# Inputs of the first two superblocks turned by VectorE inside a paired buffer, written to DRAM and read back in four parts, without TensorE transposes

## The chip, the core and the metric

The kernel runs on one core of one Trainium2 chip. The metric is device time in microseconds, of one execution: before the change 371.51 us, the median of 3 runs (371.48 to 371.51). Inputs, outputs and the reference are float32.

## What is computed

`S, D, F` are 2048, 512 and 1376. The two parts of one block, each with a normalisation that is scaled and shifted by a condition `c`:

```python
mod = (_silu(c) @ w_mod).reshape(c.shape[0], 6, 1, -1)
sa, ca, ga, sb, cb, gb = (mod[:, i] for i in range(6))
h = _layernorm(x) * (1 + ca) + sa                      # rows of 512
X = rfft2(h, axes=(-2, -1)) * (w_r + 1j * w_i)         # over S and D
x = x + ga * irfft2(X, s=(S, D), axes=(-2, -1))
h = _layernorm(x) * (1 + cb) + sb
h = einsum("bsd,df->bsf", h, w1) + b1
x = x + gb * einsum("bsf,fd->bsd", mish(h), w2)
```

## The kernel before, in words

**Stages.** The 2048 rows are held as 16 row groups: group `n` is row `p * 16 + n` on partition `p`, in `x[:, n, :]`. The Fourier part is done as dense products: forward over the row groups, then per frequency with the weights, then back. The way back has two steps for each group: `p3_col(n)` (eight products with `kc`, L830 and L831, and an evacuation by ScalarE, L833) and `p3_row(n)` (four products with `kiv`, L840, and an addition into `x` by VectorE, L843). `row_squares` and `row_scale` make the statistics of the second normalisation from it.

**The dense part.** Four groups make a superblock `i` (0 to 3) of 512 rows, two groups a block `b` (0 to 7). The rows must stand with D on the partitions, so a superblock's normalised rows are transposed. The transposed input is named by its quarters B11, B21, B12, B22 (first digit: the half of D; second: the block). It is scaled and shifted by the condition (`cols`), and each quarter is split into a high and a low half of type fp32r (`split_in`: a cast by ScalarE, L821, then a subtraction by VectorE, L822) so that three products (`TERMS`) give float32 accuracy. `up` (L962, and L945 for the 512 wide form) multiplies with the parts of `w1`, `evict` adds the bias and applies Mish, `down` (L1062) multiplies with `w2`. Superblock 0 uses plain products for most of F, the others a scheme of seven products for eight (`PRODUCTS`), whose input sums T1 to T4 are made in `sum_in`. After a block's last `down`, `gather` and `chain` (L1092 and after) put its sums into `modr`, `residual` (L1113) multiplies with the gate, and a DMA from POOL's queue adds the result into `x` in SBUF (L1114), from where `store` writes it out. `modr` is one buffer, used by one block after the other.

**How a superblock's input is turned.** `norm_one(n)` writes the normalised rows of group `n` into a buffer (ScalarE).

- Superblocks 0 and 1: `transpose_in` (L765) does four TensorE transposes against the identity `ident` into a PSUM bank, `scale_in` (L772) brings them to SBUF with scale and shift by ScalarE, two instructions of 128x256. `first_in` (L1184) and `next_in` (L1282) call these for a quarter.
- Superblocks 2 and 3: `turn_one` (L783) transposes in 32x32 blocks on VectorE into rows of `x` that are free again, `turn_out` (L787) writes this to DRAM from POOL's queue in four DMAs, `turn_in` (L794) reads it back turned through SyncE's (SP's) queue, and `scale_turned` (L798) scales it in place.

**Order.** Every engine runs its instructions in the order of the program. The steps of the back transform and of the dense part are entered in a `Plan` with a due time each, are sorted by it, and then run in the order that the table `ORDER` gives: 1155 steps before, 1187 after. The table is replaced as a whole by the change.

**Buffers and queues.** `buf(tag)` gives the next of two 128x512 buffers of that tag. DMAs are issued by SP (loads of `w1` and `w2`, sums of `w1` kept in DRAM by `keep_w1` (L735) and fetched again, turned reads, most stores), by POOL (accumulating `x<-modr`, turned writes) and a few by ScalarE. A queue's engine issues in program order, and what has to wait for data holds up what is behind it.

Of the kernel before, what the change touches and what calls it, by code (L numbers as in the profile page):

```python
# [81 lines left out]
def tile_spectral_block(ctx: ExitStack, tc: tile.TileContext, x_d, w1_d, b1_d, w2_d,  # L82
# [30 lines left out]

    def buf(tag, dt=F32):
        return work.tile([P, 512], dt, name="buf", tag=tag)
# [580 lines left out]
    even = [pm.tile([P, 512], F32, name=f"even{i}") for i in range(3)]  # L696
# [4 lines left out]
    ring, raws, src, temps, stage, turned = {}, {}, {}, {}, {}, {}  # L701
# [63 lines left out]
    def transpose_in(n, g):  # L765
        st["pt2"] = ps = bank("D")
        for k in range(2):
            for i in range(2):
                nc.tensor.transpose(ps[:, (2 * k + i) * P:(2 * k + i + 1) * P],
                                    st["h2", n + i][:, (2 * g + k) * P:(2 * g + k + 1) * P], ident)  # L770

    def scale_in(b, g, dst):  # L772
        raws[b] = dst
        ps = st.pop("pt2")
        for e in range(2):
            k = 2 * g + e
            nc.scalar.activation(dst[:, 256 * e:256 * e + 256], ps[:, 256 * e:256 * e + 256],
                                 AF.Identity, bias=cols[:, 1, 0, k:k + 1], scale=cols[:, 1, 1, k:k + 1])

# [13 lines left out]

    def turn_in(b, n, g):  # L794
        raws[b] = dst = buf("ty"["B12 B22".find(b) >= 0])
        nc.sync.dma_start(dst.rearrange("p (a s) -> p a s", a=4), turned[n][:, :, 128 * g:128 * g + 128])

    def scale_turned(b, g):  # L798
        for e in range(2):
            k, o = 2 * g + e, raws[b].rearrange("p (a k s) -> p k a s", a=4, k=2)[:, e]  # L800
            nc.scalar.activation(o, o, AF.Identity, bias=cols[:, 1, 0, k:k + 1], scale=cols[:, 1, 1, k:k + 1])
# [4 lines left out]
    def sum_in(b, dst=None):  # L806
        p, q, op = {"T1": ("B12", "B11", ALU.subtract), "T2": ("T1", "B22", ALU.subtract),
                    "T3": ("B22", "B12", ALU.subtract), "T4": ("B21", "T2", ALU.add)}[b]
        p, q = raws[p], raws[q]
        raws[b] = raws[dst] if dst in raws else dst if dst is not None else buf("h")  # L810
        nc.vector.tensor_tensor(raws[b], p, q, op=op)

    def split_in(b, i=0):
# [4 lines left out]
        if i > 1:  # L818
            r = r.rearrange("p (a m j) -> p m a j", a=4, m=4)
            h, l = (z.rearrange("p (m a j) -> p m a j", a=4, m=4) for z in (h, l))  # L820
        nc.scalar.copy(h, r)  # L821
# [50 lines left out]
    def load_w2(t, spare=None):  # L872
        st["w2", t] = rs = []
        for e, f, rows in tiles(t):
            r = buf("y")[:rows] if spare is None else spare[:, e]
# [312 lines left out]
    for n, s in ((0, 5), (1, 6), (2, 8), (3, 9)):  # L1188
        plan.at(s - N2 + 0.7, norm_one, n)
# [303 lines left out]
```

## Time and profile before

| | |
|---|---|
| median of 3 runs | 371.51 us |
| time of the profiled execution | 371.68 us |
| its span, first to last instruction | 369.9 us |
| mean granted TensorE clock | 0.998 |
| TensorE matmuls (PE), weight loads (PEld) | 361.9 us, 337.5 us |
| VectorE (DVE) | 298.3 us |
| ScalarE (ACT) | 266.8 us |
| GpSimd (POOL) | 73.9 us |
| moved by DMA | 85.76 MB |

Busy times are sums over the span of 369.9 us. They are averages over stages, so the stretches are looked at one by one: the back transform and the first superblock's input lie at 90 to 134 us, the second superblock's input is turned up to 168 us. In a row of grouped instructions stand the line of the kernel, the engine, the operation, out<-in, then durations in ns as least/median/greatest, and the first and last start. A timeline row has start, duration and count. The chain of waits has start and duration of each link. For DMA issues, "to landing" is the time from the issuing instruction to the last byte's arrival.

### The profile page before, as it was taken

What the parts mean: (1) busy time and instruction counts of PE and PEld (TensorE: products, weight loads), DVE (VectorE), ACT (ScalarE), POOL (GpSimd) and SP (SyncE); (2) the same over time, 40 slices, a digit from 0 to 9 for tenths busy, and PEclk for the clock granted to TensorE, in tenths of its full rate; (3) what the DMA queues carried; (4) which work ended last, traced back from release to release, by engine and by line L of the source; (5) the groups of instructions that cost most, each with busy time, mean ns of one, the idle gap of its engine ahead of it and who ended that gap; (6) DMA issues with size and microseconds to landing.
All of it is one profiled execution on the core that took longest, in us unless ns stands there. A gap on an engine that the chain in (4) does not pass through costs nothing. (4 is left out here: it accounts for less than half of the span.)

```text
span 369.9 us, 7822 instructions
## 1 busy us (share of the span) xinstructions
PE 361.9 (98%) x2698; PEld 337.5 (91%) x2698; DVE 298.3 (81%) x744; ACT 266.8 (72%) x601; POOL 73.9 (20%) x118
## 2 busy tenths in 40 slices
PE   8999999998999999999999999999989999999995
PEld 8999977777999999888999999999979999999994
DVE  1898967888887678989987489996749887588996
ACT  1698879996899989998757587775776654455750
POOL 0488738786000000000011210004100000000000
PEclk9999999999999999999999999999999999999999
DMA  7999997778634847657988779779896597870423
GB/s 251 381 345 378 346 371 226 230 186 307 217 115 171 257 153 221 249 196 244 259 196 265 275 246 271 239 215 280 268 232 178 170 274 265 239 269 2 116 57 113
DMA packets 49351, 85.76 MB, mean 232 GB/s; under 512 B 7169, under 2 KB 16481, under 8 KB 49057
## 3 DMA queue, kind: packets, MB, share of 16 engines
q1 hardware_dynamic: 45376, 72.56, 59.2%
q0 software_dynamic: 1776, 5.77, 7.2%
q10 hardware_dynamic: 2160, 6.95, 6.3%
q8 instruction: 21, 0.34, 0.4%
q14 instruction: 18, 0.14, 0.1%
HBM read 66.12 MB, written 15.47 MB: 221 GB/s over the span
## 5 line engine op out<-in xcount | busy, mean ns | idle before, releaser
L962 PE MATMUL bank<-hT,wr 128*128 128x256 f32 x360 | 52.3, 283 | 0.0
L1114 POOL DMA_DIRECT2D x<-modr x7 | 6.4, 918 | 206.2 <-DVE hT L822 97.4
L962 PEld LDWEIGHTS bank<-hT,wr 128*128 128x128 f32 x360 | 47.3, 192 | 0.2
L962 PE MATMUL bank<-hB,wr 128*128 128x256 f32 x318 | 45.2, 283 | 0.0
L962 PEld LDWEIGHTS bank<-hB,wr 128*128 128x128 f32 x318 | 41.5, 191 | 0.5
L888 DVE TENSOR_TENSOR al<-buf,ah 128x512 fp32r<-128x512 f32 (+1 forms) x45 | 30.0, 669 | 8.5 <-ACT ah L887 8.5
L1062 PE MATMUL bank<-w2a,ah 128*128 128x256 f32 x161 | 34.9, 283 | 0.0
L1062 PE MATMUL bank<-w2b,ah 128*128 128x256 f32 x147 | 32.2, 283 | 0.0
L887 ACT CAST ah<-buf 128x512 fp32r<-128x512 f32 (+1 forms) x45 | 26.7, 604 | 7.6 <-PE bank L1062 4.8
L1062 PEld LDWEIGHTS bank<-w2a,ah 128*128 128x128 f32 x161 | 27.0, 191 | 0.5
L1062 PEld LDWEIGHTS bank<-w2b,ah 128*128 128x128 f32 x147 | 25.1, 192 | 0.7
L830 PE MATMUL bank<-kc,d 128*128 128x128 f32 x128 | 24.8, 276 | 0.5 <-ACT d L440 0.5
L831 PE MATMUL bank<-kc,d 128*128 128x128 f32 x128 | 24.7, 275 | 0.0
L945 PE MATMUL bank<-hB,wr 128*128 128x512 f32 x96 | 24.7, 394 | 0.0
L1062 PE MATMUL bank<-w,ah 128*128 128x256 f32 x112 | 22.2, 287 | 1.1 <-DVE modr L1092 1.1
L302 PE MATMUL bank<-buf,mring 128*128 128x512 f32 x48 | 20.6, 430 | 0.2 <-DVE buf L295 0.2
L1062 PEld LDWEIGHTS bank<-w,ah 128*128 128x128 f32 x112 | 17.9, 191 | 2.5 <-DVE modr L1092 1.3
L830 PEld LDWEIGHTS bank<-kc,d 128*128 128x128 f32 x128 | 19.4, 192 | 0.7 <-ACT d L440 0.7
L945 PEld LDWEIGHTS bank<-hB,wr 128*128 128x128 f32 x96 | 17.1, 189 | 2.8
L831 PEld LDWEIGHTS bank<-kc,d 128*128 128x128 f32 x128 | 19.4, 192 | 0.0
L596 PEld LDWEIGHTS bank<-kv,a_sb 128*128 128x128 f32 x126 | 15.5, 191 | 2.7 <-issue 2.2
L790 POOL DMA_DIRECT2D turned<-x x16 | 8.9, 570 | 44.2 <-DVE x L784 31.9
(296 smaller groups left out, 1096.8 us busy)
## 6 DMA issues: line engine op xcount, KB each, us to landing
wr<-w_S SPq DMA_DIRECT2D x60, 256.0 KB, 3.8
wr<-w_A SPq DMA_DIRECT2D x45, 256.0 KB, 3.8
w_S<-hT SPq DMA_DIRECT2D x20, 256.0 KB, 2.2
x<-in_A_x_dram SPq DMA_DIRECT2D x16, 256.0 KB, 4.8
xring<-in_x_t_dram SPq DMA_DIRECT2D x16, 256.0 KB, 4.7
w_A<-wr SPq DMA_DIRECT2D x15, 256.0 KB, 2.7
x<-modr POOLq DMA_DIRECT2D x7, 512.0 KB, 5.8
out_dram<-x SPq DMA_DIRECT2D x7, 512.0 KB, 3.6
```

Source lines behind the costliest of these rows:

```text
L302: nc.tensor.matmul(pa, m[:, a, 0:128], g, start=(i == 0), stop=False)
L596: nc.tensor.matmul(pd[:, i * P:(i + 1) * P], y[:, i * P:(i + 1) * P], kv[:, 0:128], start=True, stop=True)
L790: nc.gpsimd.dma_start(t[:, a].rearrange("(c i) s -> i c s", c=4), x[32 * a:32 * a + 32, row:row + 2, :].rearrange("i r d -> i (r d)") .rea ...
L830: nc.tensor.matmul(o, dj[:, 0:128], kc[0][:, n, :], start=True, stop=False)
L831: nc.tensor.matmul(o, dj[:, 64:192], kc[1][:, n, :], start=False, stop=True)
L887: nc.scalar.copy(h, r)
L888: nc.vector.tensor_tensor(l, r, plain(h), op=ALU.subtract)
L945: nc.tensor.matmul(ups[i, t, f], ring[t, a][:, p, b, :], sides[int(a[2]) - 1][:, :, q, b, :], start=(a[2] == "1" and b == 0 and n == 0), s ...
L962: nc.tensor.matmul(o, w[:, p, k, :], h[:, q, k, :], start=(first and n == 0), stop=(last and n == 5), skip_group_check=True)
L1062: nc.tensor.matmul(out_ps[b][n][:, 256 * half:256 * half + 256], a[p][:, e], w2[t][q][:, r], start=(t == 1 and half == 0 and i == 0), stop ...
L1114: nc.gpsimd.dma_start(x[:, 2 * b:2 * b + 2, :], r, accum_op=ALU.add)
```

## The change

The tags `t` and `y` of `buf` become paired buffers: `wide(tag)` is one tile of 128x2x512, whose halves `buf` hands out in turn. The three `even` tiles become one, `evens`, so that two neighbours can be used as a pair. For superblocks 0 and 1 `transpose_in`, `scale_in`, `first_in` and `next_in` are gone. In their place:

- `turn_near(n)`: VectorE transposes the normalised group in 32x32 blocks into one half of the paired buffer of its block (`NEAR`: `wide("t")`, `evens[:, 0:2]`, `wide("t")`, `wide("y")` for the pairs 0 to 3).
- `send(n)`: POOL's queue writes that half (128x512, 256 KB) to DRAM.
- `turn_back(pair, c)`, for `c` from 0 to 3: SP's queue reads 32 partitions (32x8x128, 128 KB, in pieces of 512 bytes) back into the same paired buffer, now with D on the partitions.
- `scale_turned(b, g, True)`: ScalarE scales and shifts a quarter in place, in two instructions of 128x8x32, whose pieces of 32 elements come from a strided view (`in_order`). `split_in` and `sum_in` read the quarters through views of that kind.

Counted over the program, TensorE has 32 transposes fewer, VectorE 8 transposes (128x512) more, ScalarE the same number of scalings (16, formerly from PSUM), POOL's queue 8 DMAs more and SP's 16 more. The due times of the added steps are set in `near_in`, and the new `ORDER` moves steps on every engine throughout the dense part.

```diff
 ORDER = (
-    "3-4 0-2 16 21 5 7 15 14 73 38 8 10 71 47 9 75 80 12 32 62 6 26 17 19 13 31 24 22 69 20 23 82 11 33 124 87 27 "
...
+    "0 3-4 1-2 16 15 5 7 21 90 47 56 88 8 10 12 92 6 64 19 79 38 13 24 14 96 11 17 20 22 27 23 29 98 18 33 32 9 54 "
...
+    def wide(tag):
+        if tag not in wides:
+            wides[tag] = work.tile([P, 2, 512], F32, name="wide", tag=tag, bufs=1)
+        return wides[tag]
+
     def buf(tag, dt=F32):
+        if tag in "ty":
+            uses[tag] = uses.get(tag, 1) + 1
+            return wide(tag)[:, uses[tag] % 2]
         return work.tile([P, 512], dt, name="buf", tag=tag)
...
-    even = [pm.tile([P, 512], F32, name=f"even{i}") for i in range(3)]
+    evens = pm.tile([P, 3, 512], F32, name="even")
+    even = [evens[:, i] for i in range(3)]
...
-    def transpose_in(n, g):
-        st["pt2"] = ps = bank("D")
-        for k in range(2):
-            for i in range(2):
-                nc.tensor.transpose(ps[:, (2 * k + i) * P:(2 * k + i + 1) * P],
-                                    st["h2", n + i][:, (2 * g + k) * P:(2 * g + k + 1) * P], ident)
-
-    def scale_in(b, g, dst):
...
+    NEAR = {0: lambda: wide("t"), 1: lambda: evens[:, 0:2], 2: lambda: wide("t"), 3: lambda: wide("y")}
+
+    def turn_near(n):
+        pair = n // 2
+        if n % 2 == 0:
+            near[pair] = NEAR[pair]().rearrange("p n d -> p (n d)")
+        nc.vector.transpose(near[pair][:, n % 2 * D:n % 2 * D + D].rearrange("p (c k j) -> p c k j", c=4, k=4),
+                            st.pop(("h2", n)).rearrange("p (k c j) -> p c k j", k=4, c=4))
+
+    def send(n):
+        if n % 2 == 0:
+            turned[n] = dram.tile([2 * P, D], F32, name=f"turned{n}")
+        at = n % 2 * P
+        nc.gpsimd.dma_start(turned[n - n % 2][at:at + P], near[n // 2][:, n % 2 * D:n % 2 * D + D])
+
+    def turn_back(pair, c):
+        t = turned[2 * pair].rearrange("(m i) (c s) -> c i m s", i=32, c=4)
+        nc.sync.dma_start(near[pair][32 * c:32 * c + 32].rearrange("p (m s) -> p m s", m=8), t[c])
...
-    def scale_turned(b, g):
+    def in_order(r, near):
+        return r.rearrange("p a (k j) -> p k a j", k=2) if near else r.rearrange("p (a k s) -> p k a s", a=4, k=2)
+
+    def scale_turned(b, g, near=False):
         for e in range(2):
-            k, o = 2 * g + e, raws[b].rearrange("p (a k s) -> p k a s", a=4, k=2)[:, e]
+            k, o = 2 * g + e, in_order(raws[b], near)[:, e]
...
     def load_w2(t, spare=None):
...
-            r = buf("y")[:rows] if spare is None else spare[:, e]
+            r = wide("y")[:rows, e] if spare is None else spare[:, e]
...
-    def first_in(b, n, g):
-        transpose_in(n, g)
-        scale_in(b, g, buf("g2") if b in ("B11", "B21") else even[1 if b == "B12" else 0])
...
+    def near_in(n0, u, norms, ins, lag):
+        for n, s in enumerate(norms):
+            plan.at(u + s, norm_one, n0 + n)
+            plan.at(u + s + 0.3, turn_near, n0 + n)
+            plan.at(u + s + 0.35, send, n0 + n)
+        for n, s in zip((0, 2), ins):
+            for c in range(4):
+                plan.at(u + s + 0.01 * c, turn_back, (n0 + n) // 2, c)
+            for g in range(2):
+                plan.at(u + s + lag + 0.1 * g, scale_turned, f"B{g + 1}{n // 2 + 1}", g, True)
+
+    near_in(0, -N2, (4.7, 5.2, 7.7, 8.2), (6, 9), 1.2)
...
-            for b, n, g, s in (("B11", 0, 0, 17), ("B21", 0, 1, 18), ("B12", 2, 0, 23), ("B22", 2, 1, 25)):
-                plan.at(u + s + 0.3, next_in, b, 4 * i + n, g)
+            near_in(4, u, (17, 18, 23, 25), (19.5, 27), 3)
```

TensorE around the first `up` products, before. L840 is a row step, L830 and L831 the eight products of a column step, L962 an `up` of superblock 0 (its operand `hB` is a pair of quarters); L945 is the 512 wide `up`. The column step shown is the last one:

```order
352 L840 MATMUL bank<-kiv,buf 128x128 x4
353 L830 MATMUL bank<-kc_1104,d_756 128x128
354 L831 MATMUL bank<-kc_1132,d_756 128x128
355 L830 MATMUL bank<-kc_1104,d_756 128x128
356 L831 MATMUL bank<-kc_1132,d_756 128x128
357 L830 MATMUL bank<-kc_1104,d_756 128x128
358 L831 MATMUL bank<-kc_1132,d_756 128x128
359 L830 MATMUL bank<-kc_1104,d_756 128x128
360 L831 MATMUL bank<-kc_1132,d_756 128x128
361 L962 MATMUL bank<-hB_1283,wr 128x256 x12
362 L945 MATMUL bank<-hB_1283,wr 128x512 x3
```

The same place after, where `up` is L991 and L974 and the row step L869; row 350 is the row step of group 13, and the last column step begins at row 351:

```order
344 L860 MATMUL bank<-kc_1116,d_750 128x128
345 L991 MATMUL bank<-hB_1261,wr 128x256 x6
346 L974 MATMUL bank<-hB_1261,wr 128x512 x3
347 L991 MATMUL bank<-hB_1262,wr 128x256 x6
348 L991 MATMUL bank<-hB_1261,wr 128x256 x6
349 L974 MATMUL bank<-hB_1261,wr 128x512 x3
350 L869 MATMUL bank<-kiv,buf 128x128 x4
351 L859 MATMUL bank<-kc_1088,d_750 128x128
```

Six matmuls with B12, and after them products with B22 and B12, now stand ahead of the last column step; before, the first product with B12 stood behind it.

ScalarE at the input of superblock 0, before. L777 is a scaling out of PSUM, L821 the cast of a split, L833 the evacuation of a column step, L847 and L848 the row statistics, L726 a cast of `w1`:

```order
236 L833 COPY buf<-bank 128x512
237 L726 CAST hT_1339<-hT_1338 128x256
238 L777 ACTIVATE even_1281<-bank,cols 128x256 x2
239 L847 ACTIVATE mv<-mv 128x1
240 L848 ACTIVATE bank,mv<-x,mv 128x512
241 L833 COPY buf<-bank 128x512
242 L847 ACTIVATE mv<-mv 128x1
243 L848 ACTIVATE bank,mv<-x,mv 128x512
244 L777 ACTIVATE even_1280<-bank,cols 128x256 x2
245 L821 CAST hB_1284<-buf 128x512
246 L726 CAST hT_1339<-hT_1338 128x256
247 L821 CAST hB_1283<-even_1281 128x512
```

And after, where L825 is `scale_turned`, L850 the cast of a split, L862 the evacuation and L739 the cast of `w1`:

```order
236 L825 ACTIVATE wide<-wide,cols 128x8x32 x2
237 L862 COPY buf<-bank 128x512
238 L825 ACTIVATE wide<-wide,cols 128x8x32 x2
239 L739 CAST hT_1311<-hT_1310 128x256
240 L850 CAST hB_1261<-wide 128x512
241 L862 COPY buf<-bank 128x512
242 L825 ACTIVATE even<-even,cols 128x8x32 x2
243 L739 CAST hT_1311<-hT_1310 128x256
244 L825 ACTIVATE even<-even,cols 128x8x32 x2
245 L850 CAST hB_1262<-wide 128x512
246 L850 CAST hB_1261<-even 128x512
247 L850 CAST hB_1262<-even 128x512
```

The scalings of the four quarters stand close together behind the reads, with the four casts in among them and right behind, and the row statistics are no longer between them.

POOL's queue in the dense part, before: L1114 is a block's accumulation, L790 a turned write of superblock 2 or 3:

```order
95 L1114 DMA x<-modr 128x1024
96 L790 DMA turned_2754<-x 32x4x256 x4
97 L790 DMA turned_2959<-x 32x4x256 x4
98 L1114 DMA x<-modr 128x1024
99 L790 DMA turned_3417<-x 32x4x256 x4
100 L790 DMA turned_3504<-x 32x4x256 x4
101 L1114 DMA x<-modr 128x1024 x5
```

And after, with L805 for `send`, L1143 for the accumulation and L788 for the turned writes:

```order
96 L805 DMA turned_1432<-wide 128x512 x2
97 L805 DMA turned_1476<-even 128x512 x2
98 L805 DMA turned_1903<-wide 128x512 x2
99 L805 DMA turned_1987<-wide 128x512 x2
100 L1143 DMA x<-modr 128x1024
101 L788 DMA turned_2698<-x 32x4x256 x4
102 L788 DMA turned_2879<-x 32x4x256 x4
103 L1143 DMA x<-modr 128x1024
104 L788 DMA turned_3361<-x 32x4x256 x4
105 L1143 DMA x<-modr 128x1024
106 L788 DMA turned_3463<-x 32x4x256 x4
107 L1143 DMA x<-modr 128x1024 x4
```

Eight writes are added at the head, and the third accumulation, which stood behind all turned writes, now stands ahead of the last group of them.

More of the change, by code (lines that the diff above doesn't have):

```diff
@@ L112, in bank @@
         return psum.tile([P, 512], F32, name="bank", tag=tag)
+    wides, uses = {}, {}
+    def wide(tag):
+        if tag not in wides:
+            wides[tag] = work.tile([P, 2, 512], F32, name="wide", tag=tag, bufs=1)
+        return wides[tag]
     def buf(tag, dt=F32):
+        if tag in "ty":
+            uses[tag] = uses.get(tag, 1) + 1
+            return wide(tag)[:, uses[tag] % 2]
         return work.tile([P, 512], dt, name="buf", tag=tag)
@@ L700, in tile_spectral_block @@
     wsum = pm.tile([P, 512], F32, name="wsum")
-    ring, raws, src, temps, stage, turned = {}, {}, {}, {}, {}, {}
+    ring, raws, src, temps, stage, turned, near = {}, {}, {}, {}, {}, {}, {}
     def flat2(t):
@@ L763, in norm_one @@
         st["h2", n] = norm(n, True)
-    def transpose_in(n, g):
-        st["pt2"] = ps = bank("D")
-        for k in range(2):
-            for i in range(2):
-                nc.tensor.transpose(ps[:, (2 * k + i) * P:(2 * k + i + 1) * P],
-                                    st["h2", n + i][:, (2 * g + k) * P:(2 * g + k + 1) * P], ident)
-    def scale_in(b, g, dst):
[L773 to L778, printed above, removed]
     def turning(row):
@@ L792, in turn_out @@
                               .rearrange("i (c s) -> i c s", c=4))
+    NEAR = {0: lambda: wide("t"), 1: lambda: evens[:, 0:2], 2: lambda: wide("t"), 3: lambda: wide("y")}
[13 more added lines that the diff above has]
+        nc.sync.dma_start(near[pair][32 * c:32 * c + 32].rearrange("p (m s) -> p m s", m=8), t[c])
+        if c == 3:
+            v = near[pair].rearrange("p (m g s) -> p g m s", m=8, g=2)
+            for g in range(2):
+                raws[f"B{g + 1}{pair % 2 + 1}"] = v[:, g]
     def turn_in(b, n, g):
-        raws[b] = dst = buf("ty"["B12 B22".find(b) >= 0])
+        raws[b] = dst = wide("ty"["B12 B22".find(b) >= 0])[:, g]
         nc.sync.dma_start(dst.rearrange("p (a s) -> p a s", a=4), turned[n][:, :, 128 * g:128 * g + 128])
-    def scale_turned(b, g):
+    def in_order(r, near):
+        return r.rearrange("p a (k j) -> p k a j", k=2) if near else r.rearrange("p (a k s) -> p k a s", a=4, k=2)
+    def scale_turned(b, g, near=False):
         for e in range(2):
-            k, o = 2 * g + e, raws[b].rearrange("p (a k s) -> p k a s", a=4, k=2)[:, e]
+            k, o = 2 * g + e, in_order(raws[b], near)[:, e]
             nc.scalar.activation(o, o, AF.Identity, bias=cols[:, 1, 0, k:k + 1], scale=cols[:, 1, 1, k:k + 1])
@@ L809, in sum_in @@
         p, q = raws[p], raws[q]
-        raws[b] = raws[dst] if dst in raws else dst if dst is not None else buf("h")
+        raws[b] = raws[dst] if dst in raws else buf("h")
+        if len(p.shape) > len(raws[b].shape):
+            raws[b] = raws[b].rearrange("p (a s) -> p a s", a=8)
         nc.vector.tensor_tensor(raws[b], p, q, op=op)
@@ L820, in split_in @@
             h, l = (z.rearrange("p (m a j) -> p m a j", a=4, m=4) for z in (h, l))
+        else:
+            r = in_order(r, True)
+            h, l = (z.rearrange("p (k a j) -> p k a j", a=8, k=2) for z in (h, l))
         nc.scalar.copy(h, r)
@@ L1182, in tile_spectral_block @@
     plan.at(5.4 - N2, single_w1, False)
-    def first_in(b, n, g):
-        transpose_in(n, g)
-        scale_in(b, g, buf("g2") if b in ("B11", "B21") else even[1 if b == "B12" else 0])
-    for n, s in ((0, 5), (1, 6), (2, 8), (3, 9)):
-        plan.at(s - N2 + 0.7, norm_one, n)
-    for b, n, g, s in (("B11", 0, 0, 7), ("B21", 0, 1, 8), ("B12", 2, 0, 10), ("B22", 2, 1, 11)):
-        plan.at(s - N2 + 0.55, first_in, b, n, g)
+    def near_in(n0, u, norms, ins, lag):
[6 more added lines that the diff above has]
+                plan.at(u + s + 0.01 * c, turn_back, (n0 + n) // 2, c)
+            for g in range(2):
+                plan.at(u + s + lag + 0.1 * g, scale_turned, f"B{g + 1}{n // 2 + 1}", g, True)
+    near_in(0, -N2, (4.7, 5.2, 7.7, 8.2), (6, 9), 1.2)
     for b, key in (("B11", -6.6), ("B21", -5.6), ("B12", -0.5), ("B22", 0.6)):
@@ L1280, in tile_spectral_block @@
     plan.at(key, finish)
-    def next_in(b, n, g):
-        transpose_in(n, g)
-        scale_in(b, g, buf("ty"["B12 B22".find(b) >= 0]))
     for i in range(1, NB // 2):
@@ L1288, in tile_spectral_block @@
         if i == 1:
-            for n, s in ((0, 14.5), (1, 15.5), (2, 19.5), (3, 20.5)):
-                plan.at(u + s, norm_one, 4 * i + n)
-            for b, n, g, s in (("B11", 0, 0, 17), ("B21", 0, 1, 18), ("B12", 2, 0, 23), ("B22", 2, 1, 25)):
-                plan.at(u + s + 0.3, next_in, b, 4 * i + n, g)
+            near_in(4, u, (17, 18, 23, 25), (19.5, 27), 3)
         else:
```

86 rows, old and new, of the table ORDER are left out of this document.

## The prediction, made before the changed kernel was run

> **What bounds the kernel now.** I read the page first, then the busy time by stretches, the chain that ended last, and the instructions around the transposes.
>
> ```profile
> span 369.9 us, 7822 instructions
> PE 361.9 (98%) x2698; PEld 337.5 (91%) x2698; DVE 298.3 (81%) x744; ACT 266.8 (72%) x601; POOL 73.9 (20%) x118
> ```
>
> TensorE (PE) has work in 361.9 of 369.9 us. Where its 8.0 idle microseconds lie is in the table by stretches: first the stretch, then for each engine busy time and instructions, then granted clock, DMA share, GB/s.
>
> ```profile
> 10.00:90.00 80.00, 78.49 (x527) 65.14 (x526) 69.12 (x165) 69.24 (x163) 57.11 (x91) 1.00 0.92 311
> 90.00:134.00 44.00, 43.75 (x391) 43.75 (x392) 32.80 (x96) 38.62 (x104) 1.35 (x1) 1.00 0.57 189
> 134.00:168.00 34.00, 34.00 (x207) 29.85 (x206) 31.04 (x85) 32.34 (x78) 0.00 (x0) 1.00 0.59 199
> 168.00:184.00 16.00, 16.00 (x113) 14.96 (x112) 15.54 (x37) 12.60 (x27) 0.00 (x0) 1.00 0.90 270
> 184.00:260.00 76.00, 76.00 (x613) 74.66 (x612) 59.71 (x149) 52.64 (x108) 10.87 (x18) 1.00 0.83 251
> 260.00:280.00 20.00, 18.95 (x142) 17.77 (x141) 13.32 (x35) 14.09 (x30) 0.95 (x1) 1.00 0.86 241
> ```
>
> The columns are PE, weight loads, VectorE (DVE), ScalarE (ACT), POOL. From 90 to 260 us PE idles 0.25 us in all: there every matmul taken out should shorten the kernel by the time it holds PE, as long as nothing else comes late. But DVE and ACT are close behind. From 134 to 168 they work 31.04 and 32.34 of 34 us, so cover is thin exactly where the change adds VectorE work.
>
> The one stall behind 90 us is in 260 to 280: 20.00 - 18.95 = 1.05 us. The chain of waits names it, and the DVE timeline beside it shows what stood between.
>
> ```profile
> 267.19 7.54 DMA x<-modr
> 275.59 0.62 PE bank L1062 x3
> ```
> ```profile
> 265.26 1.22 DVE L1113 TENSOR_TENSOR modr<-modr 128x1024 f32<-128x1024 f32 x1
> 266.40 0.28 DVE L1032 TENSOR_TENSOR buf<-even 128x128 f32<-128x128 f32 x1
> 270.52 0.28 DVE L1032 TENSOR_TENSOR buf<-even,buf 128x128 f32<-128x128 f32 x1
> 274.84 0.69 DVE L1092 TENSOR_TENSOR modr<-bank,buf 128x512 f32<-128x512 f32 x1 [4.03 <-DMA x<-modr]
> ```
>
> The residual of block 2 leaves `modr` at 265.26 + 1.22 = 266.48; its accumulating DMA is done at 267.19 + 7.54 = 274.73, and only then may the chain of block 3 write `modr`. DVE had 11 instructions to do meanwhile, done by 270.80, then waited 4.03 us.
>
> **Removed: 32 transposes on PE.** They stand in seven runs of four or eight (L769). What a run costs is the distance from its start to the next matmul's start.
>
> ```profile
> 108.22 0.60 PE L769 MATMUL bank<-ident,buf 128*128 128x128 f32 x4
> 108.66 0.39 PE L830 MATMUL bank<-kc,d 128*128 128x128 f32 x2
> 152.05 0.60 PE L769 MATMUL bank<-ident,buf 128*128 128x128 f32 x4
> 152.40 0.48 PE L1062 MATMUL bank<-w,ah 128*128 128x256 f32 x2
> 155.63 0.60 PE L769 MATMUL bank<-ident,buf 128*128 128x128 f32 x4
> 155.98 0.94 PE L945 MATMUL bank<-hB,wr 128*128 128x512 f32 x3
> 163.40 1.04 PE L769 MATMUL bank<-ident,buf 128*128 128x128 f32 x8
> 164.19 0.48 PE L1062 MATMUL bank<-w2a,ah 128*128 128x256 f32 x2
> L769 PE MATMUL bank<-ident,buf x32: 270/272/273, 108.2 to 164.2; 128*128 128x128 f32 x32
> ```
>
> The four runs of superblock 0 cost 0.44 each, here read from the first; those of superblock 1 cost 0.35, 0.35 and 0.79. The sum is 4 x 0.44 + 1.49 = 3.25 us. All of it lies in stretches where PE is full, so all of it is on the path.
>
> The last row above says 272 ns for one transpose, but within a run they start 0.11 us apart: a duration is not what PE is held. [...] The starts of the next matmuls decide for 3.25.
>
> **Replaced: ACT scales, DVE turns.**
>
> ```profile
> L784 DVE STREAM_TRANSPOSE x<-buf x8: 670/704/711, 199.6 to 254.1; 128x512 f32<-128x512 f32 x8
> L801 ACT ACTIVATE buf<-buf,cols x16: 586/590/614, 217.0 to 271.2; 128x256 f32<-128x256 f32 x16
> L777 ACT ACTIVATE buf<-bank,cols x12: 545/557/580, 110.3 to 165.4; 128x256 f32<-128x256 f32 x12
> ```
>
> The 16 scalings stay on ACT but read SBUF: 16 x (590 - 557) ns = 0.5 us more. DVE gets 8 transposes x 0.704 = 5.6 us, and nothing is taken from it. From 90 to 168 us DVE then has 32.80 + 31.04 + 5.6 = 69.4 us of work and ACT 38.62 + 32.34 + 0.5 = 71.5, in 78 - 3.25 = 74.75 us of PE. Both still fit, ACT at 96%. This costs nothing as long as PE's work hides it; if the cover is gone, ACT's idle time there sets the pace (a rival below).
>
> **Added: the way through DRAM.** Eight writes on POOL's queue, sixteen reads of 128 KB on SP's. Nearest rows are those of the later superblocks, issue and landing for write and read.
>
> ```profile
> L790 POOL DMA_DIRECT2D turned<-x x16: 550/570/615, 202.2 to 256.9; - x16
> DMA to landing us min/median/max: 3.2/4.2/6.0
> L796 SPq DMA_DIRECT2D buf<-turned x8: 518/542/1406, 209.0 to 261.9; - x8
> DMA to landing us min/median/max: 3.4/4.3/5.0
> 106.81 5.41 SPq L735 DMA_DIRECT2D w_S<-hT  x2
> 133.11 1.68 PE L962 MATMUL bank<-hB,wr 128*128 128x256 f32 x12
> 104.65 1.06 PE L840 MATMUL bank<-kiv,buf 128*128 128x128 f32 x8
> 107.33 1.06 PE L840 MATMUL bank<-kiv,buf 128*128 128x128 f32 x8
> ```
> ```profile
> L843 DVE SCALAR_TENSOR_TENSOR x<-bank,x 128x512 f32<-128x512 f32 x16 | 11.0, 687 | 4.7 <-PE bank L840 4.7
> L821 ACT CAST hB<-buf 128x512 fp32r<-128x512 f32 x14 | 8.4, 614 | 0.3 <-PE bank L945 0.3
> L822 DVE TENSOR_TENSOR hB<-buf,hB 128x512 fp32r<-128x512 f32 x14 | 9.3, 685 | 1.9 <-ACT hB L821 1.8
> L726 ACT CAST hT<-hT 128x256 fp32r<-128x256 f32 x16 | 6.4, 406 | 0.0
> ```
>
> POOL has nothing else to do here (1.35 us busy in 90 to 134), so issue costs nothing. SP issues in order, and a read waits there for its two writes; behind it stand the kept weight sums, the loads of `w2` and later of `w1`, for which DVE waits. The tightest user is the first `up` with B12. In the new order it comes ahead of the last column step (the 2.68 us between the two L840 rows less the row step's 108.22 - 107.33 = 0.89, so 1.79) and of one row step more, so PE reaches it at 133.11 - 1.79 - 0.89 - 4 x 0.44 = 128.7.
>
> Now the pair n = 2, 3. DVE turns n = 3 right behind the evacuation of row step 5, which leaves PE at 107.33 + 0.89 = 108.2: 108.2 + 0.69 + 0.70 = 109.6. The write lands at 109.6 + 0.57 + 4.2 = 114.4. SP is free by then: the kept sum ahead of the reads is made just behind row step 7, two steps of 2.68 later, about 114. Four issues of 0.54 and 4.3 to landing give 120.9. ACT reaches the scaling of B12 behind column step 12. Two row steps and two column steps are left from there to that `up`, so it is at 128.7 - 2 x 2.68 = 123.3: 2.4 us of cover. From there ACT does four scalings, one cast and two splits, 4 x 0.59 + 0.41 + 2 x 0.61 = 4.0 us, and DVE one subtraction of 0.69: B12 is ready at 128.0, 0.7 us ahead of PE. So a slip of the round trip costs PE nothing up to 2.4 + 0.7 = 3.1 us and one for one beyond. With both legs at their longest (6.0 and 5.0) the slip is 2.5: still nothing. If SP is also held for 5.41 us, as it was at 106.81 by kept sums, the slip is 7.9 and PE waits 4.8. The new waits are thus between 0 and 4.8 us; I take 0.6, near the lower end, since medians leave cover and since PE's idle time in such a stretch was 0.25. Superblock 1 is left out: hundreds of instructions stand between its turns and its splits.
>
> **Moved: the stall at 275.** On DVE 25 instructions now stand between the product of block 2 and the chain of block 3 instead of 11; at the same pace, 4.4 us for 11 (266.40 to 270.80), that is 10.0 us, more than the 8.2 from 266.48 to 274.73. On POOL this accumulate is also issued ahead of the last turned writes, no longer behind them. I take the whole 1.05 as gone; bounds 0 and 1.05. The rest is rearranged everywhere without a change in its instructions; I cost that at nothing, as PE is full to the end. Below nothing it cannot gain much: idle PE time from 90 to 280 us is 0.25 + 1.05 = 1.30 us.
>
> **The sum.** The profiled execution took 371.68 us, 1.78 more than its span; the median of the runs is 371.51, 0.17 less. 371.68 - 3.25 - 1.05 + 0.6 = 367.98, and against the median 367.8.
>
> **Rivals.**
> ACT becomes the bound. It idles 78 - 70.96 = 7.0 us from 90 to 168. If its waits do not shrink with PE's work, that part lasts 71.5 + 7.0 = 78.5 us as before, only the 1.05 is won, and the time is 371.51 + 0.5 - 1.05 = 371.0. For it: 96% load, and B's splits now crowd into one place on ACT. Against: those waits were mostly for PE. In between, with 5.4 of these 7.0 us kept, it is 369.4.
>
> The round trip comes late (the slower side). Place: ACT's scaling of B12, with the evacuations of the column steps queued behind. It decides from a slip of 3.1 + 4.3 = 7.4 us on, at which all is lost. If both legs take what the slowest accumulate took (7.54) and SP is held 5.41, the slip is 3.34 + 3.24 + 5.41 = 12.0, PE waits 8.9, and the time is 371.51 - 4.30 + 8.9 = 376.1. Against: 16 writes from the same queue never took over 6.0, with DVE busy 59.71 of 76 us beside them. [...]
>
> Transposes hold PE for their whole 272 ns: 371.51 - 8.7 - 1.05 = 361.8. The start distances speak against it. [...]
>
> **Chances.** Forecast, 366.5 to 369.0: 0.66. Partly eaten by ACT or the round trip, up to 370.7: 0.12. ACT the bound, no change that can be told (within 0.2%, 0.74 us, about what a measurement of this kernel tells from none): 0.08. Late round trip, slower: 0.10. Full 272 ns: 0.04. Faster 0.66 + 0.12 + 0.04 = 0.82, same 0.08, slower 0.10. The range from 366.4 to 370.9 leaves out the last two and part of the third: it takes in no stall at all (371.51 - 4.30 = 367.2, and 0.8 for smaller waits elsewhere) and new waits of 3.7 us.
>
> **What would show it.** Right: no L769-like rows, PE idle under 0.5 us from 90 to the first `up` and near 0 to 260, no wait of DVE for `x<-modr`, the first split of B12 not waiting for a read, landings of the new DMAs within 3 to 6 us, a span near 366. Wrong: ACT waiting for a turned read in front of a scaling with PE idle behind it; SP standing for microseconds on a read; PE waiting for ACT evacuations; or a new stall at another chain.

## The result, and the profile after

The changed kernel took 368.28 us (median of 4 runs, 367.50 to 368.46), the kernel before 371.50: a ratio of 0.9917, 95% interval 0.9893 to 0.9942. The forecast was 367.8 in a range from 366.4 to 370.9. Two more sets of runs, on two chips, gave 0.9925 (0.9909 to 0.9940) and 0.9941 (0.9922 to 0.9960).

The page's first lines after the change; the profiled execution took 368.36 us, 1.76 more than its span:

```profile
span 366.6 us, 7820 instructions
PE 358.6 (98%) x2666; PEld 333.9 (91%) x2666; DVE 302.5 (83%) x752; ACT 266.9 (73%) x601; POOL 78.3 (21%) x126
```

TensorE works 3.3 us less, VectorE 4.2 more, ScalarE as long as before. The same stretches as before, with the same columns (PE, PEld, DVE, ACT, POOL, clock, DMA share, GB/s):

```profile
0.00:10.00 10.00, 8.72 (x56) 8.46 (x57) 2.54 (x12) 1.64 (x3) 0.19 (x4) 1.00 0.79 266
10.00:90.00 80.00, 78.27 (x525) 64.86 (x523) 69.04 (x165) 69.32 (x164) 57.96 (x91) 1.00 0.90 310
90.00:134.00 44.00, 43.64 (x380) 43.19 (x381) 38.75 (x109) 40.35 (x106) 2.86 (x5) 1.00 0.75 237
134.00:168.00 34.00, 34.00 (x210) 30.17 (x209) 32.11 (x87) 32.55 (x78) 2.16 (x4) 1.00 0.82 276
184.00:260.00 76.00, 76.00 (x605) 74.27 (x604) 61.16 (x155) 52.19 (x107) 11.64 (x19) 1.00 0.81 240
260.00:280.00 20.00, 20.00 (x158) 19.23 (x157) 13.98 (x31) 14.02 (x31) 0.92 (x1) 1.00 0.94 283
```

From 134 to 280 us TensorE never stands, and the stall of 1.05 us near 275 is gone. VectorE, though, now works 70.86 of the 78 us from 90 to 168 and ScalarE 72.90.

The idle times of 0.25 and 0.36 us in the stretch from 90 to 134 need care, because one wait of 0.46 us, which every kernel has at its first column step, lies across the border at 90. First before, then after:

```profile
90.25 0.49 PE L830 MATMUL bank<-kc,d 128*128 128x128 f32 x2 [0.46 <-ACT d L440]
90.01 0.49 PE L859 MATMUL bank<-kc,d 128*128 128x128 f32 x2 [0.46 <-ACT d L452]
```

Behind it, the kernel before has no wait of TensorE until the stall near 275. The changed kernel has one in this profile, and its chain of waits names the cause, a late load of `w1` (into `hT`), for which ScalarE waited:

```profile
89.62 5.95 DMA hT<-in_B_w_dram
95.59 0.71 ACT wr L739 x2
97.25 0.48 ACT buf L862
97.77 1.16 PE bank L869 x8
```

The row step at 97.77 had to wait 0.35 us for its evacuation.

Where the stall was, the DVE and POOL timelines show block 2's product, its accumulating DMA, and block 3's chain:

```profile
251.94 1.18 DVE L1142 TENSOR_TENSOR modr<-modr 128x1024 f32<-128x1024 f32 x1
253.82 0.93 POOL L1143 DMA_DIRECT2D x<-modr  x1 [1.97 <-issue]
267.72 0.68 DVE L1121 TENSOR_TENSOR modr<-bank,buf 128x512 f32<-128x512 f32 x1
```

The chain comes 13.9 us behind the DMA's issue, where it came 7.65 behind it before, and waits for nothing.

TensorE's last matmul, in the timelines of before and of after:

```profile
365.61 0.28 PE L1077 MATMUL bank<-w2b,al 96*128 96x256 f32 x1
```
```profile
361.69 0.28 PE L1106 MATMUL bank<-w2b,al 96*128 96x256 f32 x1
```

It ends 3.92 us earlier, more than the 3.70 of the forecast, but the span is only 3.3 us shorter. So 0.6 us were lost behind it. The DMA view of the span's last 2.5 us, in 40 slices, shows the last store's packets at the left; first before, then after:

```profile
DMA  9899899999999400000000000000000000000000
```
```profile
DMA  6200000000000000000000000000000500000000
q14 instruction: 1, 0.01, 1.3%
```

Before, the last packet lands 1.55 us ahead of the end (worked out from the trace's packets), after 2.32 us, and 0.6 us ahead of the end there is a load of instructions on queue q14 which the kernel before does not have there. In the records of those last microseconds SP's closing instructions are 0.4 us later than before, and POOL stands 0.34 us instead of 0.05 between two of its last, while that load runs.

The first 90 us lie ahead of the added steps and differ from trace to trace: the matmul behind the wait of 0.46 us starts at 89.60 to 90.97 us. So it is best to count from this matmul to the end of the last one. The other traces in this table are those of the experiments below:

| kernel | us from there to the end of the last matmul |
|---|---|
| before | 275.64 |
| before, without the transposes | 272.46 |
| before, block 2 added by VectorE | 275.04 |
| changed (three traces) | 271.96, 271.38, 271.39 |
| changed, without the trip | 271.38 |

In two of three traces the change took 4.26 and 4.25 us out of this part; in the first one it took out 3.68, nearly all of the difference being lost at 97 us behind the late load. There the span is 3.30 us shorter: 3.68, and 0.24 that lie ahead of this part (90.25 - 90.01), less the 0.62 behind the last matmul.

### The profile page after: what moved, and what is told of

The parts are those of the page before. It is cut to its first block, busy times and chain, and to the rows that moved or that the text cites. A ratio compares the mean times of both kernels' runs of the same rounds, so it can differ in the third digit from the quotient of the medians.

```text
span 366.6 us, 7820 instructions
## 1 busy us (share of the span) xinstructions
PE 358.6 (98%) x2666; PEld 333.9 (91%) x2666; DVE 302.5 (83%) x752; ACT 266.9 (73%) x601; POOL 78.3 (21%) x126
## 3 DMA queue, kind: packets, MB, share of 16 engines
q10 hardware_dynamic: 2160, 6.95, 6.0%
## 4 chain that ended last, share of the span: by engine, by line
PE 84%; ACT 5%; DVE 4%; DMA 2%; POOL 1%; issue 1%; ACTq 1%; SPq 0%; DVEq 0%; POOLq 0%
PE bank L1091 25%; PE bank L991 22%; PE bank L974 6%; PE bank L269 4%; PE bank L869 4%; PE bank L859 3%; PE bank L860 3%; PE bank L1037 3%; PE bank L314 3%; PE bank L1087 3%; DMA hT<-in_B_w_dram 2%; PE bank L1103 2%; PE bank L316 1%; PE bank L315 1%; PE bank L325 1%
## 5 line engine op out<-in xcount | busy, mean ns | idle before, releaser
L991 PE MATMUL bank<-hT,wr 128*128 128x256 f32 x360 | 51.6, 283 | 0.0
L991 PEld LDWEIGHTS bank<-hT,wr 128*128 128x128 f32 x360 | 47.3, 191 | 0.6
L991 PE MATMUL bank<-hB,wr 128*128 128x256 f32 x318 | 46.6, 285 | 0.0
L991 PEld LDWEIGHTS bank<-hB,wr 128*128 128x128 f32 x318 | 41.9, 191 | 0.9
L1143 POOL DMA_DIRECT2D x<-modr x7 | 6.3, 898 | 140.5 <-DVE modr L1142 84.7
L974 PE MATMUL bank<-hB,wr 128*128 128x512 f32 x96 | 24.4, 393 | 0.0
L974 PEld LDWEIGHTS bank<-hB,wr 128*128 128x128 f32 x96 | 17.3, 189 | 3.1
L788 POOL DMA_DIRECT2D turned<-x x16 | 8.9, 568 | 42.1 <-DVE x L782 42.1
```

The source lines that it names most:

```text
L974: nc.tensor.matmul(ups[i, t, f], ring[t, a][:, p, b, :], sides[int(a[2]) - 1][:, :, q, b, :], start=(a[2] == "1" and b == 0 and n == 0), s ...
L991: nc.tensor.matmul(o, w[:, p, k, :], h[:, q, k, :], start=(first and n == 0), stop=(last and n == 5), skip_group_check=True)
```

## The experiments

Theory: TensorE is the bound, so the gain is the transposes taken out of it (3.25) and the stall (1.05), and the way through DRAM lies under other work. Rivals: the gain comes from the new order; the trip is on the path; VectorE or ScalarE has become the bound. Differences are to the kernel before, or to the changed kernel, on the same chip.

**The transposes alone.** In the kernel before:

```diff
     def transpose_in(n, g):
-        st["pt2"] = ps = bank("D")
...
-                nc.tensor.transpose(ps[:, ...], st["h2", n + i][:, ...], ident)
+        st["pt2"] = st["h2", n], st["h2", n + 1]
...
-            nc.scalar.activation(dst[:, 256 * e:256 * e + 256], ps[:, 256 * e:256 * e + 256],
+            nc.scalar.activation(dst[:, 256 * e:256 * e + 256], ps[e][:, 256 * g:256 * g + 256],
```

> The kernel before, in its own order, without its 32 TensorE transposes: ScalarE scales the normalised rows straight from SBUF, so the turning is left out and nothing takes its place. Theory: TensorE is full, and the transposes held it for 3.25 us by the starts of the next matmuls, so 371.5 - 3.25 = 368.3 us, with the stall of 1.05 us near 275 still there. Rival 1, they held TensorE for their whole 272 ns each: 362.8. Rival 2, what the change won is its new order and the pace here is set by ScalarE and VectorE: 371 or more.

368.18 us beside 371.12: -2.94, ratio 0.9929 (0.9909 to 0.9949). Its busy time on the page, and the stretch with the stall:

```profile
PE 358.7 (98%) x2666; PEld 333.8 (91%) x2666; DVE 298.1 (81%) x744; ACT 267.2 (73%) x601; POOL 74.1 (20%) x118
260.00:280.00 20.00, 18.97 (x147) 18.02 (x147) 13.58 (x33) 13.87 (x29) 0.95 (x1) 1.00 0.79 230
```

TensorE works 361.9 - 358.7 = 3.2 us less, and the stall is still there (20.00 - 18.97 = 1.03). From the wait at 90 us to the last matmul it is 275.64 - 272.46 = 3.18 us shorter. So the old order gives the transposes' time back too, at about 0.10 us each. That they hold TensorE for 272 ns, 8.7 us in all, is refuted, and so is the order as the whole cause.

**The stall alone.** In the kernel before:

```diff
+            if b == 2:
+                xb = x[:, 2 * b:2 * b + 2, :]
+                nc.vector.tensor_tensor(xb, xb, r, op=ALU.add)
+            else:
+                nc.gpsimd.dma_start(x[:, 2 * b:2 * b + 2, :], r, accum_op=ALU.add)
-            nc.gpsimd.dma_start(x[:, 2 * b:2 * b + 2, :], r, accum_op=ALU.add)
```

> The kernel before, but block 2's result is added into x by VectorE (one instruction of 128x1024) and no longer by an accumulating DMA, so that block 3's chain has no DMA to wait for. Theory: the wait of 4.03 us on VectorE goes, TensorE's stall of 1.05 us with it, and the 1.2 us more of VectorE work are hidden: 371.5 - 1.05 = 370.4. Rival, another wait comes late in its place (TensorE's products there also need what ScalarE and VectorE make): 371.5.

370.42 beside 371.12: -0.70, ratio 0.9983 (0.9971 to 0.9996). The stretch, the chain on VectorE, and the one wait of TensorE behind it that the kernel before does not have:

```profile
260.00:280.00 20.00, 20.00 (x155) 19.14 (x154) 15.87 (x39) 14.31 (x30) 0.00 (x0) 1.00 0.69 221
272.85 0.69 DVE L1092 TENSOR_TENSOR modr<-bank,buf 128x512 f32<-128x512 f32 x1 [1.45 <-ACT buf L1085]
PE bank L962 <- DMA wr<-w_S: 0.5, 1, 0.5
```

The stall is gone, so the accumulating DMA was its cause. Half of what it held is given back at 303.81 us, where a fetched sum of `w1` (`wr<-w_S`) comes 0.52 us late: a stall that goes lets the next one through.

**Without the trip.** The two DMA calls in `send` and `turn_back` are taken out of the changed kernel, the rest stays:

```diff
-        nc.gpsimd.dma_start(turned[n - n % 2][at:at + P], near[n // 2][:, n % 2 * D:n % 2 * D + D])
...
-        nc.sync.dma_start(near[pair][32 * c:32 * c + 32].rearrange("p (m s) -> p m s", m=8), t[c])
```

> The changed kernel without the writes to DRAM and the reads back (8 and 16 DMAs less): the blocks of 32x32 are scaled where VectorE has left them, so the exchange between partitions is left out. Theory: the trip lies wholly under other work, so the same time as the changed kernel within 0.3 us, about 0.991 of before. Rival, the trip costs (SP standing on the reads, later loads): 0.5 to 2 us less than the changed kernel.

> The changed kernel itself beside the three others on the same chip, for the differences to it: 0.9905 to 0.9925 of before. Its profile shows whether the 0.6 us that it lost behind its last matmul in the first profile (an instruction load in the last microsecond, 1.2 us from the last store's landing to the end before and 2.0 after) come again; by the theory that they belong to the length of the program they do, by the rival that they are chance they may not.

367.40 us without the trip, 368.10 for the changed kernel beside it: 0.7 us less, against the theory at first sight. TensorE's last matmul in both:

```profile
361.71 0.28 PE L1104 MATMUL bank<-w2b,al 96*128 96x256 f32 x1
```
```profile
361.56 0.28 PE L1106 MATMUL bank<-w2b,al 96*128 96x256 f32 x1
```

TensorE is not done earlier without the trip, and from the wait at 90 us on it takes 271.38 us in both. What is shorter is the end: 1.54 us behind the last store's landing instead of 2.33 (2.32 in the first profile), and no instruction load there. (The expectation's 1.2 and 2.0 us were both read 0.3 too short.) So the trip of 24 DMAs costs no path time, and something at the end 0.8 us. Whether that is the number of instructions was put to the test from both sides, below.

**How far the trip is covered.** One or two copies more of the rows of the pair 2, 3, on POOL's queue:

```diff
         nc.gpsimd.dma_start(turned[n - n % 2][at:at + P], near[n // 2][:, n % 2 * D:n % 2 * D + D])
+        if n == 3:
+            for hop in range(1):    # 2 in the second kernel
+                t = dram.tile([2 * P, D], F32, name=f"hop{hop}")
+                nc.gpsimd.dma_start(t, turned[2])
+                turned[2] = t
```

> The changed kernel with one more leg for the rows 2 and 3 of superblock 0: behind their two writes POOL's queue copies the 512 KB once more from DRAM to DRAM, and the reads take that copy. In the changed kernel's trace the second write was issued at 111.50 and landed 3 to 3.5 us later, the reads began at 117.08 (SP had been on other work up to then) and landed by about 122.6, ScalarE scaled B12 at 124.56 and TensorE reached the product at 129.15, 0.4 us after B12's low half was ready. Theory, that cover is about 2.3 us on SP and 2.0 + 0.4 behind it: a leg of 4 to 5 us is swallowed all but 0 to 0.5 us, so 368.1 to 368.8. Rival, the trip is on the path already: 372 or more.

> The same with two copies one after the other. Theory: of 8 to 10 us the same 4.7 are swallowed and the rest is paid one for one, 371.5 to 373.5, with TensorE waiting ahead of the first product with B12 and ScalarE ahead of its scaling. Rival, the later loads on SP's queue are what is late: then TensorE waits at other products too, and longer. Rival, no cost: 368.1.

First the way of this pair in the changed kernel, from the timelines of VectorE, POOL, SP, ScalarE, VectorE and TensorE:

```profile
110.50 0.70 DVE L798 STREAM_TRANSPOSE even<-buf 128x512 f32<-128x512 f32 x1
111.50 0.54 POOL L805 DMA_DIRECT2D turned<-even  x1 [0.36 <-DVE even L798]
117.08 3.06 SPq L809 DMA_DIRECT2D even<-turned  x4
124.56 1.09 ACT L825 ACTIVATE even<-even,cols 128x256 f32<-128x256 f32 x2
128.09 1.29 DVE L851 TENSOR_TENSOR hB<-even,hB 128x512 fp32r<-128x512 f32 x2
129.15 0.96 PE L991 MATMUL bank<-hB,wr 128*128 128x256 f32 x6
```

With one copy more: POOL's copy, SP's reads, and TensorE's wait for B12's low half in the list of waits:

```profile
116.03 0.52 POOL L809 DMA_DIRECT2D hop<-turned  x1 [3.87 <-DMA turned<-even]
120.57 2.41 SPq L814 DMA_DIRECT2D even<-hop  x4
PE bank L996 <- DVE hB L856: 1.1, 1, 1.1
```

369.46 us, 1.2 to 1.4 more than the changed kernel took in the other sets. The reads slipped 120.57 - 117.08 = 3.49 us and TensorE waited 1.1: a cover of 2.4 us behind the reads, as expected (2.0 + 0.4). The expected 0 to 0.5 us was too low because POOL issued the copy only at 116.03, 0.5 us behind the write's landing, which itself came 0.8 us later than in the changed kernel (115.5 instead of 114.7). So SP's other work hid 117.08 - 116.03 = 1.05 us of the longer trip, not 2.3.

With two copies more, the reads, TensorE's wait, and the stretches behind it:

```profile
124.35 1.78 SPq L814 DMA_DIRECT2D even<-hop  x4
132.26 0.69 PE L996 MATMUL bank<-hB,wr 128*128 128x256 f32 x2 [3.14 <-ACT hB L855]
128.80:132.30 3.50, 0.36 (x4) 0.17 (x3) 1.34 (x4) 3.50 (x8) 0.00 (x0) 1.00 1.03 334
132.30:135.70 3.40, 2.86 (x9) 2.37 (x10) 3.40 (x8) 3.33 (x10) 0.00 (x0) 0.51 0.92 332
135.70:139.20 3.50, 3.50 (x15) 3.22 (x14) 3.50 (x11) 3.31 (x11) 0.00 (x0) 0.50 0.62 210
139.20:142.60 3.40, 3.40 (x30) 3.34 (x29) 1.50 (x8) 0.60 (x3) 0.00 (x0) 1.00 0.67 235
```

375.56 us, over 7 more than the changed kernel and slower than the kernel before (ratio 1.0114, 1.0093 to 1.0135). A slip of 7.27 us should cost 4.9 at most. TensorE did wait only 3.1 + 0.5 us; but then its granted clock was 0.5 for 6.8 us: the twelve products of 128x256 that start at 135.79 held it for 2.56 us, up to the next matmul at 138.35, where the same twelve held it for 1.42 us (130.65 to 132.07) at full clock in the changed kernel. Half of 6.8 and the two waits make 7.1, and from the wait at 90 us to the last matmul this trace is 6.95 us longer than the changed kernel's 271.38. That holds for the traced run (375.17 us, mean clock 0.988). The slowest of the four (376.43) has a mean clock of 0.995, by which it can have lost no more than some 2 us to the clock; what else it lost is not shown. From which gap on the clock falls is not shown: here it fell behind one of 3.14 us, and the kernel with doubled scalings below had no gap over 1.71 us and fell to 0.5 all the same.

**The end of the program.** Fewer DMA instructions for the same bytes in the changed kernel, then more of them in the kernel before:

```diff
+        else:
+            nc.gpsimd.dma_start(turned[n - 1].rearrange("(n p) d -> p n d", p=P),
+                                near[n // 2].rearrange("p (n d) -> p n d", n=2))
...
+            nc.sync.dma_start(to, w2_d[at:at + 2 * P, :].rearrange("(e p) d -> p e d", p=P))
```
```diff
     def turn_in(b, n, g):
+        for k in range(2):
+            nc.sync.dma_start(dram.tile([1, D], F32, name=f"pad{k}"), w2_d[0:1, :])
...
     def turn_out(n, row):
+        for k in range(2):
+            nc.gpsimd.dma_start(dram.tile([1, D], F32, name=f"padq{k}"), w2_d[0:1, :])
```

> The changed kernel with 4 DMA instructions fewer on POOL (both halves of a pair written by one) and 8 fewer on SP (both tiles of w2 loaded by one); the bytes are the same. In both profiles of the changed kernel about 0.75 us passed more between the last store's landing and the end than in all the others: SP and POOL stood 0.4 and 0.3 us longer in the program's last few instructions, with an instruction load beside POOL's. Theory, the queues' instruction streams have grown past a point at which one more load is needed at the end: the shorter streams lose part or all of it, 367.4 to 367.8. Rival, it has to do with what the DMAs move, or is chance: 368.1.

> The kernel before with 16 more DMA instructions on SP and 8 more on POOL, each of 2 KB from DRAM to DRAM and used by nobody, beside the turned reads and writes of superblocks 2 and 3. Theory, the length of these two streams makes the longer end: TensorE's last matmul where it was, the end 0.7 us later, 371.8 to 372.0 where the kernel before takes 371.1 to 371.5. Rival, it comes from the order or the writes of the changed kernel: no change.

> The version with 4 and 8 DMA instructions fewer once more, beside the changed kernel on the same chip. Its first profile had 0.77 us less behind the last store but TensorE had lost 0.9 us more in the first 10 us, waiting for inputs. Theory, that loss was chance and the shorter end is not: 0.5 to 0.8 us less than the changed kernel, 367.4 to 367.7. Rival, the loss at the start belongs to this version: no difference.

> The changed kernel beside the run before this one, for the difference: 368.1 to 368.3.

From the last store's landing to the end, with the records that SP and POOL left in each trace:

| kernel | SP, POOL records | us to the end |
|---|---|---|
| before | 449, 181 | 1.55 |
| changed, without the trip | 451, 182 | 1.54 |
| changed, fewer DMA instructions (twice) | 462, 193 | 1.55, 1.57 |
| before, more DMA instructions | 467, 190 | 2.04 |
| changed (three times) | 467, 198 | 2.32, 2.33, 2.31 |
| changed, turned twice (below) | 467, 198 | 2.32 |
| changed, scaled twice (below) | 469, 198 | 2.30 |
| changed, one copy more | 468, 200 | 2.33 |
| changed, two copies more | 468, 201 | 2.48 |

The end follows the length of the two streams, in either kernel. SP stands 0.35 to 0.37 us ahead of its 464th record wherever it has that many, and where that record is a drain it takes 0.12 us instead of 0.01; POOL stands 0.3 to 0.4 us ahead of its 197th. The padded kernel (before, with more DMA instructions), whose SP stream alone is that long, shows SP's part alone: 2.04 - 1.55 = 0.49. In the last three rows, with up to three records more, the waits stand that much further from the end: the place is fixed in the stream. That much is shown. What they wait for is not shown: in the changed kernel the one load of instructions on q14 there runs during POOL's wait of 0.34 us, but none is seen during SP's of 0.35, and the padded kernel has one 0.3 us ahead of its end that nobody waits for.

In the times the shorter end could not be told. The version with fewer DMA instructions took 367.89 us (ratio 0.9912, 0.9892 to 0.9931) and then 368.21 beside 368.19 for the changed kernel. Runs of both spread over 2 us. From the wait at 90 us to the last matmul the two versions do not differ (271.38 and 271.39 us in the last two profiles), so the spread of the profiled runs lies ahead of it. Part of it is visible in the first 10 us, on the same 32 matmuls, first with fewer DMA instructions, then in the changed kernel:

```profile
4.09 4.96 PE L325 MATMUL bank<-sc,wmc 128*128 128x128 f32 x32
```
```profile
4.57 3.81 PE L325 MATMUL bank<-sc,wmc 128*128 128x128 f32 x32 [0.60 <-DMA wmc<-in_w_mod_dram]
```

The second waited for its input and was still done 0.67 us earlier: from 5 to 6 us it ran 12 matmuls and the first 7, which came to 12 a microsecond only from 7 us on. In these two profiled runs (367.52 and 367.53 us) that takes back most of the 0.74 us that the shorter end gives. The padded kernel took 373.43 us, 2.4 over the kernel before, of which its trace (the fastest of its runs, 372.04) shows 0.5; the rest is open.

**How much cover is left.** Each near transpose, or each near scaling, done twice in the changed kernel:

```diff
+        for again in range(2):
+            nc.vector.transpose(near[pair][:, n % 2 * D:n % 2 * D + D].rearrange("p (c k j) -> p c k j", c=4, k=4), h)
```
```diff
+            for again in range(2 if near else 1):
+                nc.scalar.activation(o, o, AF.Identity, bias=cols[:, 1, 0, k:k + 1], scale=cols[:, 1, 1, k:k + 1])
```

> The changed kernel with each of the 8 new VectorE transposes done twice into the same place: 8 x 0.70 = 5.6 us more on VectorE. From 90 to 168 us VectorE worked 70.9 of 78 us in the changed kernel, so 76.5 would still fit. Theory, what is left of VectorE's cover is thin: the four of superblock 0 delay its additions into x by 0.7 us each between 104 and 112 us, and TensorE pays 0.3 to 1.5 us, 368.5 to 369.7. Rival, all hidden: 368.2.

> The changed kernel with the 16 scalings of superblocks 0 and 1 done twice (the second scaling changes the values): 16 x 0.59 = 9.4 us more on ScalarE. From 90 to 134 us ScalarE worked 40.4 and from 134 to 168 us 32.6 us; with 4.7 more in each it would need 45.1 of 44 and 37.3 of 34. Theory, ScalarE is close behind TensorE as the prediction had it, and becomes the bound: 3 to 5 us more, 371 to 373. Rival, ScalarE's order leaves room that the sums don't show: 368.2 to 369.5.

Both cost more than expected: 372.23 and 377.01 us beside 368.19. TensorE's waits in the first, and in the second the two largest with the clock behind them:

```profile
PE bank L975 <- DVE wr L740: 1.9, 2, 1.6
PE bank L870 <- DVE x L873: 1.0, 1, 1.0
```
```profile
PE bank L992 <- ACT hB L851: 3.4, 2, 1.7
PE bank L870 <- DVE x L873: 1.6, 1, 1.6
134.00:136.00 2.00, 2.00 (x7) 1.78 (x8) 2.00 (x6) 1.94 (x7) 0.00 (x0) 0.50 0.68 262
```

5.6 us more on VectorE cost 4.0 us, 9.4 more on ScalarE cost 8.8. (In the profiled run of the second, at 378.74 us, some 1.7 of it went by half a clock for 3.4 us; a run at 375.79 had a mean clock of 0.999, so the clock is not most of it.) So the changed kernel has little cover left on either engine. The 5.6 us that the change itself added to VectorE were free: from the wait at 90 us on the changed kernel takes 271.38 us, and the kernel before without transposes, less its stall of 1.03, takes 271.43. The next 5.6 are paid at 70%. Whether ScalarE had more cover before the change was not tried.

## Why the prediction was right, and where not

- **PE full, so removed matmuls count.** Right. The starts of the next matmuls gave 3.25 us; the kernel without transposes was 3.18 shorter from the wait at 90 us on, the change 3.2 when the stall is taken off (4.26 - 1.05). The duration of 272 ns would have given 8.7.
- **The stall at 275.** Right: 1.05 gone, by the distance of product and chain (14.6 us from the product's end, where 10.0 was estimated).
- **New waits 0.6.** Right in size in the first profile (4.26 - 3.68 = 0.58) by luck: they came at 97 us from a late load of `w1`, which the forecast did not name, and not at B12. In the other two profiles there are none. The 0.25 us of idle time that it leaned on was part of the wait of 0.46 us at the border of the stretch; behind that the kernel before had none up to the stall. The path through DRAM ran 0.7 to 2.7 us later than estimated step by step (turned at 111.2 instead of 109.6, reads from 117.1 instead of 114.4, because SP's kept sum was later; scaling at 124.6 instead of 123.3), but TensorE came later too, at 129.15 instead of 128.7, and B12 was ready 0.4 us ahead of it (0.7 estimated).
- **ACT and DVE as cover.** Right for this change, but the margin was read wrongly. Sums over 78 us left ScalarE 4% and VectorE 7%; yet of the microseconds added later 70% were paid on VectorE and over 90% on ScalarE. Idle time in these stretches was not cover where TensorE waited for what came behind it (1.9 and 1.0 us with the turns done twice, 3.4 and 1.6 with the scalings done twice).
- **The late round trip.** The mechanism and its place are shown, with a cover of 2.4 us instead of 3.1. Its price was mis-sized: "one for one beyond" left out the clock, which took about half of what the traced run lost. A slip of 7.27 us behind the reads' real start cost over 7 us against the changed kernel, not 4.2, so all is lost somewhere between slips of 3.5 and 7.3. The 5.41 us for which it let SP be held is a row of two issues with the wait between them; the wait is 4.75.
- **What was missing.** The sum had no term for the end of the program. It costs 0.62 us of span (0.77 behind the last store), more than the whole miss of 368.28 - 367.8 = 0.48. In traces without the late load at 97 us the waits that never came (0.6) and the longer end cancel, which is luck again.

## What to carry to other kernels

Cost a removed matmul by the start of the next one, in a stretch where TensorE has no gaps, and not by its duration (here 0.10 us, not 272 ns); then look which engine's result comes last there, since its idle sum is not its cover. The transfer through DRAM was free here while it had microseconds to spare (2.4 behind the reads); past that, look at the granted clock too, which here fell to 0.5 behind a gap of 3.14 us. Look at the last 2 us as well: 24 DMA instructions more lengthened the end of the program by 0.77 us here, though they cost nothing on the path. And compare traces from a fixed matmul on, so that a start that differs from run to run drops out.

## What the runs showed of the hardware

- 32 fp32 transposes of 128x128 in runs of four and eight held TensorE for 0.10 us each (3.18 us in all), with rows of 272 ns.
- After a gap of 3.14 us TensorE's granted clock was 0.5 for 6.8 us; behind two gaps of 1.61 and 1.71 us, whose ends lie 4.6 us apart, it was 0.5 for 3.4 us, while behind a single gap of 1.69 us in the same trace it stayed full.
- SP stood 0.36 us ahead of its 464th record and POOL 0.3 us ahead of its 197th, at the program's end, where streams of 462 and 193 records had no such wait.
- Eight writes from POOL's queue took 539 to 779 ns to issue and 3.0 to 5.2 us to land, beside a VectorE that worked 70.86 of 78 us.
